# The low parts of W1 in an attention and mixture-of-experts kernel: subtractions on GpSimd in place of ScalarE copies and adding DMAs, for seven of sixteen halves

## The chip, the cores and the metric

The kernel runs on one core of a Trainium2 chip. The metric is the device time of one execution in microseconds (us); less is better. A core has five engines that run side by side, each with its own queue of instructions in a fixed order: TensorE (PE; PEld are its weight loads), VectorE (DVE), ScalarE (ACT), GpSimd (POOL) and SyncE (SP, which here only issues DMAs). SBUF is the on-chip memory that all of them read, PSUM the small one into which PE writes its sums, HBM the large one outside. DMAs issued by SP and by GpSimd go through different queues.

## The reference

Two parts follow each other. First a gated linear attention over 4 batches, 8 heads, 768 steps and 48 channels, then a mixture of 8 experts over the 3072 rows of 384 numbers that it gives. Tokens are assigned to experts greedily in the order of their logits, 384 to each expert:

```python
state = alpha[:, :, t, :, None] * state + np.einsum('bhd,bhe->bhde', k[:, :, t], v[:, :, t])
y[:, :, t] = np.einsum('bhd,bhde->bhe', q[:, :, t], state)
...
for e in range(E):
    mask = assigned == e
    h = np.maximum(x[mask] @ w1[e], 0.0)
    out[mask] = h @ w2[e]
```

W1 of an expert is 384 x 1024, W2 is 1024 x 384, all float32.

## The kernel before

The first 150 us are the attention and the first routing step. The change lies in what follows, the experts.

**The loop.** Experts are served in the order in which they fill up. Below they are called expert 0 to expert 7 by that order (i in the code), so "expert 1" is the second. Each has 8 blocks of 128 hidden units (q, `FB` = 8), in two halves of four: (i, 0) and (i, 1). `ffn1` (line 1056) computes a block's h from x and W1, nine matmuls; ScalarE then writes `hh`, the rounded positive part (line 1066), and VectorE `hl`, what the rounding left (line 1067). `ffn2` (line 1072), two blocks behind, multiplies both by W2 into `y`, nine matmuls.

**High and low parts.** PE takes float32 numbers here in a rounded form (`F32R`). So each weight half is split in two (`split`, line 977): a high part, the rounded copy, and a low part, the raw weight less the high part. Products are high by high, high by low and low by high. The tiles are `w1hi`, `w1lo`, `w2hi`, `w2lo`; each W1 half is 128 x 3 x 512, each W2 half 128 x 4 x 384, 768 KB both. ScalarE writes the high parts, two copies to a half (line 1005). The low parts come in two steps: ScalarE writes the *negated* rounded weight into `w1lo` or `w2lo`, and a DMA issued by GpSimd adds the raw weight to it in place (`low`, line 989, with `accum_op=OP.add`). Only the first half, (0, 0), has its `w1lo` from GpSimd's own subtraction, in four pieces of 128 columns (line 1023).

**The search.** While expert i is computed, the next expert's tokens are searched (`search`, line 712): five or six levels, each of them a chain from VectorE to PE and back. In a level VectorE makes `nd` (line 779) and `cmp` (line 683), PE counts with short matmuls into `rt` (lines 745 to 751), VectorE makes `need` and `gt` (lines 757 to 764), PE sums once more (line 772), VectorE takes `k` (line 776). At the end of a search stands a run of small VectorE operations (`q`, `ab`, `qe` and others through line 790), up to `sums`; then `extract` (line 914) makes the token indices `idx` (line 956), and GpSimd issues three gathers of rows, `xr` (line 963). PE transposes the rows into `xt` (line 1046), ScalarE copies them to `xh`, VectorE makes `xl`.

**What sets the order.** A scheduler puts the program into one order for each engine, from its own costs, and every engine keeps to it: PE waits at a search matmul even if the next expert matmul is ready, and a GpSimd instruction that waits holds all behind it. `tc.issue_after(x)` adds that an instruction comes after x on its queue. Rotating buffers bound how far ahead things go: three halves of each split tile, two experts of raw weights, five `yt` tiles for the stores of `y`, which GpSimd issues (line 1094).

## Time and profile before

| | |
|---|---|
| median of 3 runs | 412.92 us (411.97 to 413.25) |
| the profiled execution | 413.29 us, its span 411.6 us |
| clock granted to PE, mean | 0.991 |
| busy of the span: PE, DVE, ACT, POOL | 94%, 69%, 52%, 45% |
| instructions in the profile | 9897 |
| moved by DMA | 88.05 MB, of which 33.83 MB by GpSimd's queue |

The span is what the trace covers, from the first instruction to the last; what lies around it makes up the difference to the execution's time. A row of the timeline has the start in us from the span's begin, the duration in us, engine, line and operation, then written tile <- read tiles, shape and count; a bracket at its end tells how long the engine was idle before it and what ended that. A row of a group has count, busy time in us and mean ns. Rows of before carry the line numbers of the kernel before. Durations on GpSimd overlap each other somewhat: the next instruction's start is recorded before the one in front has ended.

### The profile page before, as it was taken

To read this page: it belongs to the slowest core of one execution; us is meant where nothing else is said; L and a number is where in the kernel's file an instruction comes from. 1 tells how busy PE (TensorE), PEld (TensorE's weight loads), DVE (VectorE), ACT (ScalarE), POOL (GpSimd) and SP (SyncE) were. 2 spreads that over 40 slices of the span, in tenths; PEclk is the share of its full clock that TensorE was granted. 3 is DMA by queue.
4 is the path that set the end of the run, shared out by engine and by line. 5 is a ranking of instruction groups with operands and counts; after the bars stand their busy time and mean duration, and the time that the engine had idled before them with its cause. 6 is when DMAs were issued, how large, how long until landed. Compare 5 with 4: busy or idle time off the path is not lost.

```text
span 411.6 us, 9897 instructions
## 1 busy us (share of the span) xinstructions
PE 385.0 (94%) x3775; PEld 340.6 (83%) x3775; DVE 283.3 (69%) x909; ACT 214.5 (52%) x382; POOL 186.8 (45%) x230
## 2 busy tenths in 40 slices
PE   6899999999999888898999998999999999999992
PEld 3788889887888556797798997899998999999992
DVE  8889997899994686687586796597796872312210
ACT  3456555654553015626639629529529539478211
POOL 5899988566851016213405506216126263614102
PEclk9899999999999999999999999999999999999998
DMA  8989898763020148789799999979999999999601
GB/s 274 378 284 309 276 311 230 245 200 105 22 79 30 50 151 204 164 204 262 206 220 323 200 282 274 213 252 278 210 298 226 197 303 327 247 305 202 155 0 58
DMA packets 43711, 88.05 MB, mean 214 GB/s; under 512 B 3856, under 2 KB 18192, under 8 KB 43664
## 3 DMA queue, kind: packets, MB, share of 16 engines
q0 software_dynamic: 11408, 33.83, 38.9%
q1 hardware_dynamic: 32256, 53.60, 38.5%
q8 instruction: 29, 0.48, 0.5%
q14 instruction: 18, 0.15, 0.1%
HBM read 53.59 MB, written 9.44 MB: 153 GB/s over the span
## 4 chain that ended last, share of the span: by engine, by line
PE 48%; DVE 16%; issue 15%; DMA 14%; POOL 3%; ACT 1%; POOLq 0%; SPq 0%; DVEq 0%
PE h L1062 12%; PE y L1082 11%; DMA w1r<-in_moe_w_dram 4%; PE xt L421 4%; PE y L484 4%; DMA w1lo<-w1r 4%; PE y L477 4%; PE s L433 4%; DMA xr<-x_dram,idx 3%; DMA w2lo<-w2r 3%; DVE te L393 3%; PE lg L502 2%; DVE tp L399 2%; PE rt L751 1%; PE st L445 1%
## 5 line engine op out<-in xcount | busy, mean ns | idle before, releaser
L1066 ACT ACTIVATE hh<-h 128x384 fp32r<-128x384 f32 x64 | 31.3, 488 | 85.3 <-PE h L1062 62.5
L1067 DVE SCALAR_TENSOR_TENSOR hl<-h,hh 128x384 fp32r<-128x384 f32 x64 | 35.4, 553 | 51.0 <-ACT hh L1066 50.7
L1082 PE MATMUL y<-w2hi,hh 128*128 128x384 f32 x192 | 66.6, 347 | 0.0
L1082 PE MATMUL y<-w2lo,hh 128*128 128x384 f32 x192 | 65.8, 343 | 0.4 <-DMA w2lo<-w2r 0.4
L1082 PE MATMUL y<-w2hi,hl 128*128 128x384 f32 x192 | 65.3, 342 | 0.0
L1094 POOL DMA_INDIRECT out_dram<-yt,idx x24 | 25.5, 1062 | 50.5 <-ACT yt L1087 46.8
L1062 PE MATMUL h<-xh,w1lo 128*128 128x384 f32 x192 | 46.9, 343 | 0.0
L1062 PE MATMUL h<-xh,w1hi 128*128 128x384 f32 x192 | 46.0, 342 | 0.6 <-ACT xh L1049 0.6
L1062 PE MATMUL h<-xl,w1hi 128*128 128x384 f32 x192 | 45.8, 342 | 0.0
L993 POOL DMA_DIRECT2D w1lo<-w1r x15 | 20.3, 1350 | 55.7 <-ACT w1lo L1005 40.1
L963 POOL DMA_INDIRECT xr<-x_dram,idx x24 | 26.2, 1092 | 40.4 <-DVE idx L956 26.2
L1062 PEld LDWEIGHTS h<-xh,w1hi 128*128 128x128 f32 x192 | 33.9, 188 | 4.4 <-issue 2.9
L403 POOL TENSOR_TENSOR kh<-rk,te 128x512 f32<-128x512 f32 (+1 forms) x24 | 29.4, 1226 | 17.1 <-DVE z L413 11.4
L1082 PEld LDWEIGHTS y<-w2lo,hh 128*128 128x128 f32 x192 | 36.3, 189 | 0.7 <-DMA w2lo<-w2r 0.7
L1082 PEld LDWEIGHTS y<-w2hi,hh 128*128 128x128 f32 x192 | 36.3, 189 | 0.0
L1082 PEld LDWEIGHTS y<-w2hi,hl 128*128 128x128 f32 x192 | 36.2, 189 | 0.1
L1062 PEld LDWEIGHTS h<-xl,w1hi 128*128 128x128 f32 x192 | 33.8, 189 | 0.5 <-DVE xl L1051 0.2
L1062 PEld LDWEIGHTS h<-xh,w1lo 128*128 128x128 f32 x192 | 33.9, 189 | 0.4 <-DMA w1lo<-w1r 0.3
L1005 ACT ACTIVATE w1hi<-w1r 128x768 fp32r<-128x768 f32 x32 | 26.8, 840 | 10.4 <-DMA w1r<-in_moe_w_dram 8.0
L435 ACT ACTIVATE sm<-s 128x1024 f32<-128x1024 f32 x24 | 24.6, 1026 | 13.9 <-PE s L433 13.4
L399 DVE TENSOR_TENSOR_SCAN tp<-al,z 128x512 f32<-128x512 f32 (+1 forms) x26 | 29.6, 1138 | 2.6 <-DVE z L413 0.5
L393 DVE TENSOR_TENSOR_SCAN te<-al,z 128x511 f32<-128x511 f32 (+2 forms) x26 | 30.8, 1186 | 0.5
(204 smaller groups left out, 833.8 us busy)
## 6 DMA issues: line engine op xcount, KB each, us to landing
w1r<-in_moe_w_dram SPq DMA_DIRECT2D x16, 768.0 KB, 7.7
w2r<-in_moe_w_dram SPq DMA_DIRECT2D x16, 768.0 KB, 10.0
w2lo<-w2r POOLq DMA_DIRECT2D x16, 768.0 KB, 10.4
w1lo<-w1r POOLq DMA_DIRECT2D x15, 768.0 KB, 8.0
al<-in_alpha_dram SPq DMA_DIRECT2D x24, 260.0 KB, 4.1
rk<-in_k_dram SPq DMA_DIRECT2D x24, 256.0 KB, 4.2
rq<-in_q_dram SPq DMA_DIRECT2D x24, 256.0 KB, 4.4
rv<-in_v_dram SPq DMA_DIRECT2D x24, 192.0 KB, 3.9
```

The lines of the kernel that those rows point to most:

```text
L393: nc.vector.tensor_tensor_scan(te.t[:, lo:top][:, ::-1], al.t[:, lo + 1:top + 1][:, ::-1], zb[:, lo + 1:top + 1][:, ::-1], al.t[:, 4 * C + ...
L399: nc.vector.tensor_tensor_scan(tp.t[:, lo:hi], al.t[:, lo:hi], zb[:, lo:hi], 1.0, op0=OP.mult, op1=OP.add)
L403: eng.tensor_tensor(out_.t[:, us].rearrange("p u c -> p (u c)"), x.t[:, lo:hi], f.t[:, lo:hi], op=OP.mult)
L435: add(A_, 1.05, lambda: nc.scalar.activation(sm.t, sc.t, AF.Copy), r=[(sc, 0), (sc, 1)], w=[sm])
L963: gathers[b] = last_gather[0] = nc.gpsimd.indirect_dma_start(out=XR[i][:, b], out_offset=None, in_=x_dram, in_offset=bass.IndirectOffsetOn ...
L993: return nc.gpsimd.dma_start(x.bitcast(F32), raw_, accum_op=OP.add, max_dma_last_dim=8192)
L1005: nc.scalar.activation(dst, src, AF.Copy, scale=scale)
L1062: F1[i, q] = nc.tensor.matmul(o, a[:, d], x[:, d], start=(n == 0), stop=(n == 3 * DB - 1))
L1066: HA[i, q] = nc.scalar.activation(hh, o, AF.Relu)
L1067: HL[i, q] = nc.vector.scalar_tensor_tensor(hl, o, 0.0, hh, op0=OP.max, op1=OP.subtract)
L1082: F2[i, q] = nc.tensor.matmul(Y[b], a[:, bs], w, start=(q == 0 and n == 0), stop=(q == FB - 1 and n == 2))
L1094: st_ = nc.gpsimd.indirect_dma_start(out=out, out_offset=bass.IndirectOffsetOnAxis(ap=IDX[i][:, b:b + 1], axis=0), in_=yt, in_offset=None)
```

## The change

A table `SUBTRACTED` names the halves whose `w1lo` is subtracted on GpSimd: (0, 0) as before, and now both halves of expert 1 and the first halves of experts 2 to 6. For those seven new halves ScalarE no longer writes the negated copy (two copies each) and no adding DMA for `w1lo` is issued; GpSimd subtracts four pieces each instead. The adding DMA for `w2lo` is issued between the second and the third piece (for (0, 0) ahead of the first, as before). The first piece comes after the latest issued gather in GpSimd's queue. The second halves of experts 2 to 6 and both halves of expert 7 stay with copies and DMAs.

```diff
+    SUBTRACTED = ((0, 0), (1, 0), (1, 1), *((i, 0) for i in range(2, E - 1)))
...
+        subtracted = (i, hf) in SUBTRACTED
...
-            copies(n, (hi1[ix_], w1r[ix_], 1.0), *([(lo1[ix_], w1r[ix_], -1.0)] * (not first)))
+            copies(n, (hi1[ix_], w1r[ix_], 1.0), *([(lo1[ix_], w1r[ix_], -1.0)] * (not subtracted)))
...
-        if first:
-            x = low(lo2, w2r)
+        if subtracted:
+            x = None
             for j in range(FB // 2):
+                if j == (0 if first else FB // 4):
+                    with tc.issue_after(x.ins) if x is not None else ExitStack():
+                        x = low(lo2, w2r)
                 c = slice(j * 128, (j + 1) * 128)
-                with tc.issue_after(x.ins):
+                with tc.issue_after((x or last_gather[0]).ins):
                     x = nc.gpsimd.tensor_sub(lo1[:, :, c], w1r[:, :, c], hi1[:, :, c])
         else:
             low(lo1, w1r)
```

The change also moves instructions on the engines. Three places follow. GpSimd's queue at expert 1, before: the gathers of expert 1 (`xr_2691`), the two adding DMAs of (1, 0), three stores of expert 0, the two adding DMAs of (1, 1), the gathers of expert 2.

```order
L963 DMA xr_2691<-x_dram_62,idx_2685 128x384 x3
L993 DMA w1lo_2697<-w1r_2641 128x3x512
L993 DMA w2lo_2699<-w2r_2642 128x1536
L1094 DMA out_0_dram<-yt_2770,idx_2185 3072x384
L1094 DMA out_0_dram<-yt_2775,idx_2185 3072x384
L1094 DMA out_0_dram<-yt_2780,idx_2185 3072x384
L993 DMA w1lo_2835<-w1r_2641 128x3x512
L993 DMA w2lo_2837<-w2r_2642 128x1536
L963 DMA xr_3179<-x_dram_62,idx_3173 128x384 x3
```

And the same place now (the lines of the changed kernel are some five further on):

```order
L964 DMA xr_2691<-x_dram_62,idx_2685 128x384 x3
L1028 TENSOR_TENSOR w1lo_2697<-w1r_2641,w1hi_2696 128x3x128 x2
L995 DMA w2lo_2699<-w2r_2642 128x1536
L1028 TENSOR_TENSOR w1lo_2697<-w1r_2641,w1hi_2696 128x3x128 x2
L1028 TENSOR_TENSOR w1lo_2836<-w1r_2641,w1hi_2835 128x3x128 x2
L1099 DMA out_0_dram<-yt_2771,idx_2185 3072x384
L1099 DMA out_0_dram<-yt_2776,idx_2185 3072x384
L1099 DMA out_0_dram<-yt_2781,idx_2185 3072x384
L995 DMA w2lo_2838<-w2r_2642 128x1536
L1028 TENSOR_TENSOR w1lo_2836<-w1r_2641,w1hi_2835 128x3x128 x2
L964 DMA xr_3181<-x_dram_62,idx_3175 128x384 x3
```

Two subtractions now stand ahead of each w2lo issue; the first two of (1, 1) stand ahead of expert 0's stores, the last two behind w2lo of (1, 1) and ahead of expert 2's gathers.

GpSimd's queue at expert 3, before (`xr_3655` are expert 3's gathers, `w1lo_3680` and `w2lo_3682` the half (3, 0), the last two rows the half (3, 1)):

```order
L1094 DMA out_0_dram<-yt_3267,idx_2685 3072x384
L993 DMA w1lo_3680<-w1r_3601 128x3x512
L963 DMA xr_3655<-x_dram_62,idx_3649 128x384 x3
L993 DMA w2lo_3682<-w2r_3602 128x1536
L993 DMA w1lo_3798<-w1r_3601 128x3x512
L993 DMA w2lo_3800<-w2r_3602 128x1536
```

And now:

```order
L1099 DMA out_0_dram<-yt_3270,idx_2685 3072x384
L964 DMA xr_3658<-x_dram_62,idx_3652 128x384 x3
L1028 TENSOR_TENSOR w1lo_3683<-w1r_3604,w1hi_3682 128x3x128 x2
L995 DMA w2lo_3685<-w2r_3605 128x1536
L1028 TENSOR_TENSOR w1lo_3683<-w1r_3604,w1hi_3682 128x3x128 x2
L995 DMA w1lo_3802<-w1r_3604 128x3x512
L995 DMA w2lo_3804<-w2r_3605 128x1536
```

The adding DMA of (3, 0) stood ahead of the gathers; its place is taken by subtractions behind them. The same holds at expert 4; at experts 2, 5 and 6 the gathers stood first already.

PE's queue at the start of expert 1, before: the third block of transposes, a search matmul, and at once the first blocks of h (`y_2315` is a block of expert 0's result).

```order
L1082 MATMUL y_2315<-w2hi,hl 128x384
L1046 MATMUL xt<-ident,xr 128x128 x3
L772 LDWEIGHTS one_84
L772 MATMUL rt<-gt_108,one_84 128x8
L1062 MATMUL h<-xh,w1hi 128x384 x4
L1062 MATMUL h<-xl,w1hi 128x384 x3
```

And now:

```order
L1051 MATMUL xt<-ident,xr 128x128 x3
L1087 MATMUL y_2315<-w2hi,hh 128x384
L1087 MATMUL y_2315<-w2lo,hh 128x384
L1087 MATMUL y_2315<-w2hi,hl 128x384
L1087 MATMUL y_2313<-w2hi,hh 128x384
L1067 MATMUL h<-xh,w1hi 128x384 x6
```

The third block of transposes stands some twelve matmuls earlier, with four matmuls of expert 0's y between it and the first h; between the second transposes and the next count of the search there are now 18 instead of 14 expert matmuls. On ScalarE the copies of the seven halves close up: at expert 2 the order `w1hi`, `w1lo`, `w1hi`, `w1lo`, `hh` becomes `w1hi`, `w1hi`, `w2lo`, `hh`. VectorE and SP have the same instructions, SP in the same order.

## The prediction

> **What bounds the kernel now.** First the page for its totals, then the busy time by stage from 191 us, where expert 1 begins. Columns: stretch, its length, then busy time of PE, PEld, DVE, ACT and POOL, the clock, the DMA share.

> ```profile
> PE 385.0 (94%) x3775; PEld 340.6 (83%) x3775; DVE 283.3 (69%) x909; ACT 214.5 (52%) x382; POOL 186.8 (45%) x230
> 191.00:225.00 34.00, 32.12 (x273) 29.24 (x271) 24.48 (x88) 19.45 (x33) 11.65 (x11) 1.00 0.96 243
> 225.00:258.00 33.00, 30.94 (x240) 28.10 (x238) 24.57 (x101) 20.09 (x33) 12.15 (x11) 1.00 1.05 251
> 258.00:400.00 142.00, 141.98 (x968) 133.96 (x969) 76.63 (x296) 80.92 (x137) 48.52 (x44) 1.00 0.93 231
> ```

> The matmuls bound every stage: from 258 to 400 us PE is busy 141.98 of 142 us. So removed ScalarE copies (ACT 52% busy) or GpSimd issues are worth nothing by themselves. What can be won are the holes of PE between 191 and 258 us, 1.88 us of them in the first row and 2.06 in the second. The timeline of PE names them; the bracket is the idle time before a row and what ended it.

> ```profile
> 196.99 0.98 PE L1062 MATMUL h<-xh,w1hi 128*128 128x384 f32 x4 [0.57 <-ACT xh L1049]
> 201.66 0.44 PE L1082 MATMUL y<-w2lo,hh 128*128 128x384 f32 x1 [0.42 <-DMA w2lo<-w2r]
> 221.11 0.17 PE L772 MATMUL rt<-gt,one 128*128 128x8 bf16 x1 [0.88 <-DVE gt L764]
> 252.65 0.17 PE L772 MATMUL rt<-gt,one 128*128 128x8 bf16 x1 [0.42 <-DVE gt L764]
> 257.90 1.02 PE L1046 MATMUL xt<-ident,xr 128*128 128x128 f32 x6 [1.64 <-DMA xr<-x_dram,idx]
> ```

> They add up to 3.93 us. Each ends in something that the change touches; the rest of this text takes them in turn, and then asks which new holes come.

> **The change part by part.** It removes 14 ScalarE copies and 7 adding DMAs, and adds 28 subtractions on GpSimd.

> ```profile
> L1005 ACT ACTIVATE w1lo<-w1r 128x768 fp32r<-128x768 f32 x30 | 25.1, 836 | 0.0
> 157.74 4.25 POOL L1023 TENSOR_TENSOR w1lo<-w1r,w1hi 128x384 fp32r<-128x384 f32 x4
> L1023 POOL TENSOR_TENSOR w1lo<-w1r,w1hi 128x384 fp32r<-128x384 f32 x4 | 4.3, 1364 | 0.0
> ```

> ScalarE loses 14 x 0.836 = 11.7 us. GpSimd loses seven issues. Its four present subtractions end 4.25 us after the first starts, and one alone takes 1.36, so each further one adds (4.25 - 1.36) / 3 = 0.96 us; 28 add 27 us. GpSimd is 45% busy and stays off the path in sum; its order matters, below. The low parts themselves come sooner, but none of PE's holes above ends in w1lo: worth 0.

> *The hole at 257.90.* It is the longest, and it is GpSimd's queue that makes it.

> ```profile
> 249.26 0.17 DVE L956 SCALAR_TENSOR_TENSOR idx<-xt,other 64x3 int32<-64x3 f32 x1
> 249.34 1.33 POOL L993 DMA_DIRECT2D w1lo<-w1r  x1 [13.84 <-ACT w1lo L1005]
> 250.98 1.07 POOL L963 DMA_INDIRECT xr<-x_dram,idx  x1 [0.30 <-issue]
> w1lo<-w1r POOLq DMA_DIRECT2D x1, 768.0 KB, 8.0
> xr<-x_dram,idx POOLq DMA_INDIRECT x3, 6.0
> 308.40 1.60 POOL L963 DMA_INDIRECT xr<-x_dram,idx  x1 [7.28 <-DVE idx L956]
> xr<-x_dram,idx POOLq DMA_INDIRECT x3, 3.6
> ```

> The first four rows are expert 3's (the last column of a DMA row is the median time to landing), the other two the gathers of expert 5. Expert 3's indices are ready at 249.43, but the adding DMA stands ahead of the three gathers, and lands at 249.34 + 8.0 = 257.3; the first gather lands just behind it, when the hole ends. Now the gathers go first, some 1.3 us sooner, with no 768 KB ahead of them in their queue. Where nothing of that kind was ahead, at expert 5, three gathers took 3.6 us in the median instead of 6.0. Landing then falls near 255, before PE wants them at 257.90 - 1.64 = 256.26. I take all 1.64; the low end is 0.9, if the weight loads in flight slow them as they do expert 2's.

> *221.11 and 252.65.* Both are VectorE's: ahead of the comparison `gt` stands `hl`, which waits for ScalarE's `hh`, and `hh` stands behind four copies.

> ```profile
> 218.88 0.83 ACT L1005 ACTIVATE w1lo<-w1r 128x768 fp32r<-128x768 f32 x1
> 219.61 0.47 ACT L1066 ACTIVATE hh<-h 128x384 fp32r<-128x384 f32 x1
> 220.12 0.56 DVE L1067 SCALAR_TENSOR_TENSOR hl<-h,hh 128x384 fp32r<-128x384 f32 x1 [1.08 <-ACT hh L1066]
> 251.65 0.56 DVE L1067 SCALAR_TENSOR_TENSOR hl<-h,hh 128x384 fp32r<-128x384 f32 x1 [1.23 <-ACT hh L1066]
> 224.85 0.82 PE L1046 MATMUL xt<-ident,xr 128*128 128x128 f32 x6
> 219.69 0.99 POOL L963 DMA_INDIRECT xr<-x_dram,idx  x1 [0.30 <-issue]
> xr<-x_dram,idx POOLq DMA_INDIRECT x3, 5.3
> ```

> In the new order two low copies go and one w2lo copy comes ahead of that `hh`: one copy less, 219.61 - 218.88 = 0.73 us. At 252.65 that covers the 0.42. At 221.11 it covers 0.73 of 0.88, but the next thing PE needs is expert 2's gathers: the middle one, issued at 219.69, landed 5.3 us later, at 225.0, and PE's transposes began at 224.85 with no hole. Coming 0.73 sooner, PE waits there for about 0.5. So 0.2 to 0.3 net; I take 0.3 (ends 0 and 0.73).

> *196.99 and 201.66.* The first two rows below belong to w2lo's late landing, the third gives PE's pace.

> ```profile
> 187.89 1.42 POOL L993 DMA_DIRECT2D w1lo<-w1r  x1 [1.06 <-ACT w1lo L1005]
> 190.46 0.92 POOL L993 DMA_DIRECT2D w2lo<-w2r  x1 [1.15 <-ACT w2lo L1005]
> 188.16 0.68 PE L1082 MATMUL y<-w2hi,hl 128*128 128x384 f32 x3
> ```

> PE's new order puts expert 1's third block of transposes four y matmuls ahead of the first h, and ScalarE has two copies fewer before `xh`. The present hole is the wait for `xh`, 0.57. Three such matmuls take 0.68 us, so four cover the 0.57 (low end 0). The w2lo's ScalarE copies come two places sooner, two subtractions stand ahead instead of an issue, and w1lo's transfer is no longer in front: issued between 189 and 190.6, landing well before 201.2: 0.42 (low end 0.2).

> Gains: 1.64 + 0.3 + 0.42 + 0.57 + 0.42 = 3.35 us (ends 1.2 and 3.93).

> *What it adds: holds of VectorE.* The search for the next expert alternates between VectorE and PE, in a fixed order. While GpSimd reads two tensors, VectorE's operations on two tensors seem to stand:

> ```profile
> 86.42 1.27 POOL L403 TENSOR_TENSOR qh<-rq,tp 128x512 f32<-128x512 f32 x1
> 86.51 1.20 DVE L568 TENSOR_TENSOR key<-m,sg 128x12 int32<-128x12 int32 x1
> L863 DVE TENSOR_TENSOR key<-m,sg 128x24 int32<-128x24 int32 x4 | 0.7, 176 | 0.0
> 161.63 0.41 DVE L779 SCALAR_TENSOR_TENSOR nd<-dig,k 128x24 bf16<-128x24 bf16 x1
> ```

> The tiny `key` took 1.20 us beside GpSimd's product and ended with it; its larger sibling alone takes 0.176. `nd` at 161.63 lies under the last present subtraction and ends 0.05 us behind it (157.74 + 4.25 = 161.99). [...]

> In each search level only `nd` and `cmp` read two SBUF tensors (`need`, `gt`, `hl` and `k` have an operand in PSUM, and I take them as free), so the question is whether they meet a subtraction. The subtractions stand behind the gathers, two, one DMA issue, two. For expert 5:

> ```profile
> 311.58 0.95 POOL L963 DMA_INDIRECT xr<-x_dram,idx  x1 [0.30 <-issue]
> 313.82 0.24 DVE L779 SCALAR_TENSOR_TENSOR nd<-nd,k,dig 128x24 bf16<-128x24 bf16 x1
> 314.10 0.56 DVE L683 TENSOR_TENSOR cmp<-nd,iota 128x768 bf16<-128x768 bf16 x1
> 314.74 0.44 PE L745 MATMUL rt<-o,cmp 128*128 128x32 bf16 x8
> 317.14 0.24 DVE L779 SCALAR_TENSOR_TENSOR nd<-nd,k,dig 128x24 bf16<-128x24 bf16 x1
> ```

> The gathers' issues end at 312.53; the first two subtractions run to 312.53 + 2 x 0.96 = 314.45, the other two from about 315.4 to 317.3. `nd` at 313.82, 0.24 us long here against the 0.41 above, is held 0.6 us; PE reads `cmp` 0.08 us after its end, so the hole is nearly 0.6. The next `nd`, moved to 317.7, is clear. The same reckoning from the indices of experts 2, 3 and 4 gives holds of up to 0.5, 0 and 0.2, of which expert 2's lies under its wait for the gathers: 0 together, high end 1.0 each. For (1, 0) the long hold falls on a `cmp` that PE does not want before the gathers land; two later ones meet a level that now has four more matmuls in front: 0.2. For (1, 1) the last two subtractions come behind w2lo's issue and meet the dense end of a search:

> ```profile
> 206.50 0.89 POOL L993 DMA_DIRECT2D w2lo<-w2r  x1 [2.23 <-ACT w2lo L1005]
> 208.83 0.23 DVE L790 TENSOR_SCALAR q<-nd,k 128x24 f32<-128x24 bf16 x1
> ```

> With the 0.99 us of the two earlier holes gone, the issue stands at 205.5, the subtractions behind it at 206.4 to 208.3, and `q`, with several operations on two SBUF tensors after it, at 207.8: held 0.5 (ends 0 and 1.9). Expert 6's four come when VectorE has only the last choice left, with slack in PE's order: 0. Holds: 0.6 + 0.2 + 0.5 = 1.3 us (ends 0 and 5.8, a full subtraction in each of six halves).

> Queued behind the subtractions are the w2lo adding DMAs (1 to 2 us later than without them, about as the w1lo issues held them before) and expert 0's three stores, behind two subtractions that wait for ScalarE; the ring of five yt tiles covers those, and no engine waits for a store before the end.

> Sum: 3.35 - 1.3 = 2.05 us less. The profiled execution took 413.29 us, 0.37 above the median of 412.92; from the median: 410.9.

> **The rivals.** *Holds cost nothing:* VectorE slips between the subtractions. For it: the holds foreseen are few and hang on tenths of a microsecond. Against: the 1.20 us row. All of the holes go: 412.92 - 3.9 = 409.0. *The holes move:* the gathers of experts 2 and 3 land as late as now, since the DMA share is 0.96 and 1.05 in those two stages, so PE only reaches them sooner; 0.57 + 0.42 remain won, against 1.3 of holds: 412.92 + 0.3 = 413.2. *Slower by holds:* the phases fall worse by half a microsecond, and a full subtraction holds `nd` in each of the six halves from (1, 0) to (5, 0): 5.8 - 3.35 = 2.5 more, 415.4. It decides from 3.35 / 0.96, that is when more than three of the six are hit in full. For it: PE reads `cmp` 0.08 us behind its end, so there is no slack to take a hold up; against it: the rhythm worked out above. [...]

> **How the numbers follow.** Forecast 0.45, nothing from the holds 0.2, moved holes 0.2, slower 0.15. The forecast's own ends (gain 1.2 to 3.93, holds 0 to about 3) put a fifth of it within 1.2 us of no change. The range runs from 408.5, half a microsecond (the runs' own spread) below the best case, to 415.0, which takes in the moved holes and part of the slower case. 0.3% (1.2 us) is about what a measurement of this kernel can tell from no change. Faster: 0.36 + 0.2, with a little of the moved holes: 0.57; same 0.24; slower 0.19.

> **What would show it.** In the changed profile the rows at 257.90 and 252.65 lose their brackets, expert 3's gathers come directly behind `idx`, and expert 2's transposes gain a wait of about 0.5. `nd` and `cmp` rows beside the subtractions grow from 0.24 to up to 1.2 us, at expert 5 and at the end of the search within (1, 1), with a PE wait on `cmp` or `sums` right after. Wrong it is if no such row grows, if gathers still end PE's longest hole, or if such rows appear at every expert.

## The result, and the profile after

The changed kernel took 430.01 us (median of 4 runs, 429.25 to 432.85), the kernel before, run beside it, 413.09 us (411.97 to 413.71): a ratio of 1.0425, 95% interval 1.0373 to 1.0478. It is 4% slower, where 410.9 us was forecast and 415.0 was the upper end. The profiled execution of after took 429.72 us with a span of 427.4, 15.8 us longer than before's 411.6. Here and below, medians are over all executions of a kernel, while ratios leave out those more than 1.5% above the fastest of the same kernel.

Of the page of after, the busy time of PE and the row with the granted clock in 40 slices (10.7 us each; 9 is full):

```profile
PE 392.9 (92%) x3775; PEld 347.5 (81%) x3775; DVE 297.8 (70%) x909; ACT 205.6 (48%) x368; POOL 205.3 (48%) x251
...
PEclk9699999999999999999998998899999899999998
```

PE has the same 3775 matmuls and is busy 7.9 us longer with them; besides, it is idle for longer. The clock row tells where the first comes from: 8s from the 22nd slice on. The timeline of PE in after names the idle time, between 186 and 400 us:

```profile
191.21 0.55 PE L1051 MATMUL xt<-ident,xr 128*128 128x128 f32 x3 [1.23 <-DMA xr<-x_dram,idx]
192.40 0.96 PE L749 MATMUL rt<-o,cmp 128*128 128x8 bf16 x24 [0.64 <-DVE cmp L684]
221.38 0.17 PE L773 MATMUL rt<-gt,one 128*128 128x8 bf16 x1 [0.44 <-DVE gt L765]
225.91 0.57 PE L752 MATMUL rt<-o,cmp 128*128 128x16 bf16 x12 [2.68 <-DVE cmp L684]
264.38 0.44 PE L746 MATMUL rt<-o,cmp 128*128 128x32 bf16 x8 [2.87 <-DVE cmp L684]
298.12 0.44 PE L746 MATMUL rt<-o,cmp 128*128 128x32 bf16 x8 [2.74 <-DVE cmp L684]
330.65 0.44 PE L746 MATMUL rt<-o,cmp 128*128 128x32 bf16 x8 [2.87 <-DVE cmp L684]
```

The five holes of before are gone, or halved in the case of `gt` at 221. In their place stand four new ones, one at each of the experts 2 to 5, all ended by the same thing: `cmp`, the search's comparison on VectorE. They add up to 11.16 us. What VectorE and GpSimd did ahead of the one at 298.12, in order of time:

```profile
292.69 0.56 DVE L1072 SCALAR_TENSOR_TENSOR hl<-h,hh 128x384 fp32r<-128x384 f32 x1
292.70 2.00 POOL L1028 TENSOR_TENSOR w1lo<-w1r,w1hi 128x384 fp32r<-128x384 f32 x2
294.31 0.88 DVE L780 SCALAR_TENSOR_TENSOR nd<-nd,k,dig 128x24 bf16<-128x24 bf16 x1
294.63 1.02 POOL L995 DMA_DIRECT2D w2lo<-w2r  x1
295.22 2.84 DVE L684 TENSOR_TENSOR cmp<-nd,iota 128x768 bf16<-128x768 bf16 x1
295.27 2.36 POOL L1028 TENSOR_TENSOR w1lo<-w1r,w1hi 128x384 fp32r<-128x384 f32 x2
```

`nd` meets the tail of the first pair of subtractions and takes 0.88 us instead of 0.24. The w2lo issue stands between the pairs, but `nd` ends only when half of it is over, and `cmp` follows at once: it begins 0.05 us ahead of the second pair, which runs to 297.63, and ends at 298.06. It is held through both subtractions, not through one. `hl` at 292.69 lies beside a subtraction too and takes its usual 0.56 us; it reads one of its two tensors from PSUM. The rows that group all comparisons of this shape, first before, then after:

```profile
L683 DVE TENSOR_TENSOR cmp<-nd,iota 128x768 bf16<-128x768 bf16 x16 | 8.9, 557 | 0.5
```

```profile
L684 DVE TENSOR_TENSOR cmp<-nd,iota 128x768 bf16<-128x768 bf16 x16 | 15.8, 988 | 0.5
L1072 DVE SCALAR_TENSOR_TENSOR hl<-h,hh 128x384 fp32r<-128x384 f32 x64 | 35.4, 554 | 47.2 <-ACT hh L1071 46.8
```

The 16 comparisons take 6.9 us more in all, three times 2.3; the fourth held one, at expert 2, has another shape. The busy time by stretch shows the second price, behind each of the four holes (last three columns: clock, DMA share, GB/s):

```profile
225.91:230.00 4.09, 4.09 (x28) 3.71 (x28) 1.73 (x6) 0.10 (x1) 3.03 (x3) 0.58 0.98 192
264.38:270.40 6.02, 6.02 (x27) 5.62 (x28) 2.85 (x10) 0.98 (x2) 2.21 (x3) 0.50 1.07 190
298.12:302.10 3.98, 3.98 (x25) 3.87 (x26) 1.75 (x8) 0.77 (x2) 1.75 (x2) 0.62 1.06 192
330.65:336.00 5.35, 5.34 (x34) 4.74 (x35) 2.41 (x10) 1.22 (x2) 1.75 (x2) 0.68 1.07 191
```

PE is busy all the time there, at a clock of 0.50 to 0.68; before had 1.00 from 258 to 400. What is lost is the length times the missing share: 1.7 + 3.0 + 1.5 + 1.7 = 7.9 us. The sum: 11.2 of holes, 7.9 of clock and 0.64 for the small hole at 192.40, less the 3.5 us of holes that went (0.57 + 0.42 + 0.42 + 1.64, and 0.88 - 0.44), makes 16.2 us; the span grew by 15.8. (Expert 3's gathers would be in time without PE's new delays too: in e3 below, where no long hole comes before them, PE does not wait for them either.)

The theory to be tested was: while GpSimd subtracts, reading two tensors, VectorE's operations that read two tensors from SBUF stand until the row of subtractions ends; PE, which has the search's matmul next in its order, idles; and an idle time of that length drops the granted clock, to the 0.50 to 0.68 of the rows above. The rivals: the new orders of PE and ScalarE; late transfers; any work of GpSimd; expert 1's own holds as the trigger.

### The profile page after: what moved, and what is told of

Read it like the earlier page. It is cut to its first block, busy times and chain, and to the rows that moved or that the text cites. A ratio compares the mean times of both kernels' runs of the same rounds, so it can differ in the third digit from the quotient of the medians.

```text
span 427.4 us, 9908 instructions
## 1 busy us (share of the span) xinstructions
PE 392.9 (92%) x3775; PEld 347.5 (81%) x3775; DVE 297.8 (70%) x909; ACT 205.6 (48%) x368; POOL 205.3 (48%) x251
## 4 chain that ended last, share of the span: by engine, by line
PE 63%; DVE 18%; issue 8%; DMA 4%; ACT 3%; POOL 1%; SPq 1%; POOLq 0%; DVEq 0%; ACTq 0%
PE y L1087 19%; PE h L1067 19%; DVE cmp L684 4%; PE xt L422 4%; PE y L485 4%; PE y L478 4%; PE s L434 4%; PE lg L503 2%; DVE te L394 2%; PE rt L752 2%; DVE tp L400 1%; DMA w1r<-in_moe_w_dram 1%; DMA al<-in_alpha_dram 1%; PE xt L1051 1%; PE st L446 1%
## 5 line engine op out<-in xcount | busy, mean ns | idle before, releaser
L1087 PE MATMUL y<-w2hi,hh 128*128 128x384 f32 x192 | 68.3, 356 | 0.0
L1087 PE MATMUL y<-w2lo,hh 128*128 128x384 f32 x192 | 67.8, 353 | 0.0
L1087 PE MATMUL y<-w2hi,hl 128*128 128x384 f32 x192 | 67.5, 353 | 0.0
L1099 POOL DMA_INDIRECT out_dram<-yt,idx x24 | 24.1, 1002 | 65.9 <-ACT yt L1092 63.0
L1067 PE MATMUL h<-xh,w1lo 128*128 128x384 f32 x192 | 47.1, 345 | 0.0
L1067 PE MATMUL h<-xh,w1hi 128*128 128x384 f32 x192 | 46.9, 347 | 0.0
L1067 PE MATMUL h<-xl,w1hi 128*128 128x384 f32 x192 | 46.3, 345 | 0.0
L404 POOL TENSOR_TENSOR kh<-rk,te 128x512 f32<-128x512 f32 (+1 forms) x24 | 29.4, 1225 | 17.4 <-DVE z L414 11.8
L1087 PEld LDWEIGHTS y<-w2hi,hl 128*128 128x128 f32 x192 | 37.6, 196 | 0.1
L1087 PEld LDWEIGHTS y<-w2lo,hh 128*128 128x128 f32 x192 | 37.5, 195 | 0.0
L1087 PEld LDWEIGHTS y<-w2hi,hh 128*128 128x128 f32 x192 | 37.5, 195 | 0.0
L684 DVE TENSOR_TENSOR cmp<-nd,iota 128x768 bf16<-128x768 bf16 (+4 forms) x36 | 36.6, 1027 | 1.1
L1028 POOL TENSOR_TENSOR w1lo<-w1r,w1hi 128x384 fp32r<-128x384 f32 x32 | 35.8, 1226 | 2.5 <-ACT w1hi L1007 2.4
L1067 PEld LDWEIGHTS h<-xh,w1hi 128*128 128x128 f32 x192 | 34.3, 191 | 2.5 <-issue 1.6
L1067 PEld LDWEIGHTS h<-xl,w1hi 128*128 128x128 f32 x192 | 34.2, 191 | 0.5 <-DVE xl L1056 0.2
L1067 PEld LDWEIGHTS h<-xh,w1lo 128*128 128x128 f32 x192 | 34.4, 191 | 0.1
L437 POOL TENSOR_SCALAR_AFFINE_SELECT sm<-sm 128x1024 f32<-128x1024 f32 x24 | 26.2, 1092 | 11.5 <-ACT sm L436 11.1
## 6 DMA issues: line engine op xcount, KB each, us to landing
w1r<-in_moe_w_dram SPq DMA_DIRECT2D x16, 768.0 KB
w2r<-in_moe_w_dram SPq DMA_DIRECT2D x16, 768.0 KB
w2lo<-w2r POOLq DMA_DIRECT2D x16, 768.0 KB
w1lo<-w1r POOLq DMA_DIRECT2D x8, 768.0 KB
```

What stands on the lines that cost most here:

```text
L404: eng.tensor_tensor(out_.t[:, us].rearrange("p u c -> p (u c)"), x.t[:, lo:hi], f.t[:, lo:hi], op=OP.mult)
L437: add(G_, 1.15, lambda: nc.gpsimd.affine_select(sm.t, sm.t, pattern=[[0, 8], [1, C]], compare_op=OP.is_ge, fill=0.0, base=0, channel_multi ...
L684: nc.vector.tensor_tensor(words(dst, nt, js), keyed(d, nt, js), each(iotas[t], nt, js), op=OP.is_ge)
L1028: x = nc.gpsimd.tensor_sub(lo1[:, :, c], w1r[:, :, c], hi1[:, :, c])
L1067: F1[i, q] = nc.tensor.matmul(o, a[:, d], x[:, d], start=(n == 0), stop=(n == 3 * DB - 1))
L1087: F2[i, q] = nc.tensor.matmul(Y[b], a[:, bs], w, start=(q == 0 and n == 0), stop=(q == FB - 1 and n == 2))
```

## The experiments

The kernel before ran beside each group of them, on other chips, where its median was 415.1 to 417.1 us; ratios are against those runs.

**Expert 1 alone (e1).**

```
-SUBTRACTED = ((0, 0), (1, 0), (1, 1), *((i, 0) for i in range(2, E - 1)))
+SUBTRACTED = ((0, 0), (1, 0), (1, 1))
```

> The subtractions of expert 1's two halves stay, those of experts 2 to 6 go back to copies and adding DMAs. Theory (VectorE's comparisons are held while GpSimd subtracts, experts 2 to 5): the four holes of 2.7 to 2.9 us and the slow clock behind them go; the forecast gains at 196.99 and 201.66 (0.57 + 0.42) and part of 221.11 (0.3) stay, so 411 to 413 us, against 413.1 before. Rival A (the new order of the first experts' work on PE and ScalarE costs the time): most of the 17 us stays, 425 us or more. Rival B (expert 1's own holds, where one VectorE operation took 2.72 instead of 0.35 us, set off the rest): some 3 to 5 us stay, 416 to 418.

Measured: 0.9987 (0.9935 to 1.004), the four holes gone. What is left on PE of its kind is 0.49 us at expert 1:

```profile
190.60 0.56 PE L749 MATMUL rt<-o,cmp 128*128 128x8 bf16 x12 [0.49 <-DVE cmp L684]
...
251.94 0.17 PE L773 MATMUL rt<-gt,one 128*128 128x8 bf16 x1 [0.96 <-DVE gt L765]
256.64 0.55 PE L1051 MATMUL xt<-ident,xr 128*128 128x128 f32 x3 [1.12 <-DMA xr<-x_dram,idx]
```

The new order of the first experts' work is not the cause. Nor does a gain stand clear of the noise (the interval reaches from 2.7 us less to 1.7 more): the `gt` hole and the gathers' hole of expert 3 are still there, since its adding DMA stands ahead of the gathers again.

**All but expert 1 (e9).**

```
+SUBTRACTED = ((0, 0), *((i, 0) for i in range(2, E - 1)))
```

> The changed kernel without the subtractions of expert 1's two halves (copies and adding DMAs there); those of experts 2 to 6 stay. Theory: the four holes stay, with what follows them, 15 to 19 us above before: 429 to 436 on a chip where before takes 413 to 417. Rival (the holes of experts 2 to 5 are set off by expert 1's held operation, 2.72 us at 187.49, or by its new order): most of the loss goes, 420 or less.

Measured: 1.0417 (1.0346 to 1.0488), with holes of 2.72, 2.93, 2.72 and 2.92 us. Two of them:

```profile
264.46 0.43 PE L746 MATMUL rt<-o,cmp 128*128 128x32 bf16 x8 [2.93 <-DVE cmp L684]
...
328.37 0.44 PE L746 MATMUL rt<-o,cmp 128*128 128x32 bf16 x8 [2.92 <-DVE cmp L684]
```

The whole loss sits in experts 2 to 6; the two runs together rule out expert 1 as its cause or trigger.

**One tensor instead of two (e3).**

```
-x = nc.gpsimd.tensor_sub(lo1[:, :, c], w1r[:, :, c], hi1[:, :, c])
+x = nc.gpsimd.tensor_scalar(lo1[:, :, c], hi1[:, :, c], 0.0, None, op0=OP.mult)   # halves of experts 1 to 6
```

> The changed kernel with each of its 28 new subtractions replaced by w1hi times 0.0 (GpSimd reads one tensor from SBUF instead of two; W1's low parts of those halves come out as zero, so part of the product is left out). Every engine's order stays that of the changed kernel. Theory (two tensors read by GpSimd and two by VectorE hold each other): the held comparisons fall from 2.8 to 3.8 us back to 0.55 to 0.95, the four holes and the slow clock go, 410 to 412 us. Rival (any GpSimd operation on SBUF holds them): 425 to 430. Rival (order, late transfers): 430, nothing changes.

Measured: 0.9957 (0.9913 to 1.0), no hole on PE over 1.34 us between 186 and 400 us. Comparisons and GpSimd's new operations in this run, then a comparison that lies wholly beside a pair of them:

```profile
L684 DVE TENSOR_TENSOR cmp<-nd,iota 128x768 bf16<-128x768 bf16 x16 | 10.1, 632 | 0.5
L1028 POOL TENSOR_SCALAR w1lo<-w1hi 128x384 fp32r<-128x384 f32 x28 | 37.3, 1448 | 1.5 <-ACT w1hi L1007 1.3
...
284.06 0.74 DVE L684 TENSOR_TENSOR cmp<-nd,iota 128x768 bf16<-128x768 bf16 x1
283.48 2.70 POOL L1028 TENSOR_SCALAR w1lo<-w1hi 128x384 fp32r<-128x384 f32 x2
```

GpSimd works longer than in after, at the same places of the same queue, and with the same order of instructions on every other engine; the comparisons take 0.63 us on average instead of 0.99. So it is not the order, not the transfers and not GpSimd's being busy; what went is GpSimd's reading of a second tensor from SBUF. One thing stays open: the edit also makes the operation another instruction, a multiplication by a number instead of a subtraction of tensors, and no run tells the count of tensors from the kind of instruction. The run also gives an estimate of what the change would have won without the holds: 0.0043 x 415.9 = 1.8 us (0 to 3.6).

**Three in a row (e4).**

```
-if j == (0 if first else FB // 4):
+if j == (0 if first else 1 if i > 1 else FB // 4):
```

> The changed kernel with the w2lo issue of experts 2 to 6 behind the first subtraction instead of the second, so that one subtraction stands alone and three follow each other. Theory (a comparison that meets a row of subtractions is held to the end of the last): it now ends 0.4 to 0.6 us behind the third, some 0.3 to 1 us later than behind the second: each of the four holes 3.0 to 3.9 us, 431 to 435 us. Rival (it is held only by the subtraction during which it began): holes of 1 us or less, 417 to 422.

Measured: 1.0274 (1.0158 to 1.0391), 430.32 us against 430.01 of after on its own chip; holes of 1.79, 2.90, 2.94 and 3.11. At expert 3, VectorE, GpSimd and PE:

```profile
258.72 3.78 DVE L684 TENSOR_TENSOR cmp<-nd,iota 128x768 bf16<-128x768 bf16 x1
258.76 3.31 POOL L1028 TENSOR_TENSOR w1lo<-w1r,w1hi 128x384 fp32r<-128x384 f32 x3
262.55 0.44 PE L746 MATMUL rt<-o,cmp 128*128 128x32 bf16 x8 [2.90 <-DVE cmp L684]
```

The comparison is held through all three, 3.78 us, and ends 0.43 us behind the third. The rival, one subtraction at most, is out. The time did not rise with it, against the expectation of up to 5 us more; that the ratio lies below after's 1.0425 shows no gain either, since it rests on three runs between 425.6 and 430.7 us and the two intervals overlap. In the trace the three begin sooner, so that the hole grows by 0.03 to 0.24 us only at experts 3 to 5, and at expert 2, where `cmp` meets the single one first, it is 0.89 us shorter.

**A break between them (e5).**

```
+if i > 1 and j % 2:
+    with tc.issue_after(x.ins):
+        x = nc.gpsimd.memset(lo1[:, :, c].bitcast(F32), 0.0)
 with tc.issue_after((x or last_gather[0]).ins):
     x = nc.gpsimd.tensor_sub(lo1[:, :, c], w1r[:, :, c], hi1[:, :, c])
```

> The changed kernel with a GpSimd memset (it only writes) between the two subtractions of each pair of experts 2 to 6; nothing else moves on any engine. Theory (a comparison is held by GpSimd's reading of two tensors as long as such operations follow each other without a break): it gets through at the memset, so it is held by one subtraction, about 1 us instead of 2.3; the holes shrink to some 1.0 to 1.5 us, TensorE's clock stays at 1.00 behind them as it did behind the hole of 1.64 us of before, and the time is 413 to 419 us. Rival (the operation that was held waits until GpSimd has done all that is queued, or a writing operation holds it as well): holes of 3 us or more, 430 to 436.

Measured: 1.0121 (1.0035 to 1.0207), that is a median of 421.5 us on this chip, and by the ratio 5 us above before (1.5 to 8.6); some two thirds of the loss are gone. At expert 4, GpSimd and VectorE, then PE's two longest waits for `cmp`:

```profile
287.09 1.96 DVE L780 SCALAR_TENSOR_TENSOR nd<-nd,k,dig 128x24 bf16<-128x24 bf16 x1
287.63 1.36 POOL L1031 TENSOR_TENSOR w1lo<-w1r,w1hi 128x384 fp32r<-128x384 f32 x1
288.57 0.78 POOL L1029 MEMSET w1lo<- 128x384 f32 x1
...
289.70 0.44 PE L746 MATMUL rt<-o,cmp 128*128 128x32 bf16 x8 [1.50 <-DVE cmp L684]
320.45 0.43 PE L746 MATMUL rt<-o,cmp 128*128 128x32 bf16 x8 [2.37 <-DVE cmp L684]
```

The held operation ends at 289.05, with the single subtraction (288.99), while the memset still runs (288.57 to 289.35): here an operation that only writes lets VectorE through. The holes are 1.5 us where one subtraction is met and 2.37 where `nd` meets one and `cmp` the next; of these it was only the longest behind which the clock fell. The time lies 2 us above the end of what the theory gave, 419; before itself takes 4 us longer on this chip than on that of after, so the difference says nothing about that hole.

**One expert (e6).**

```
+SUBTRACTED = ((0, 0), (4, 0))
```

> The kernel before with subtractions for the first half of one expert only, the fifth (number 4), in the place where the changed kernel has them. Theory (each expert pays by itself: a hole of some 2.7 us, and 1.5 to 3 us of clock at 0.50 behind it): 4 to 6 us above before, one hole. Rival (the loss needs the whole reordered stretch, or holes that follow each other): no change within 1 us, or more than 10 us.

Measured: 1.0089 (1.0048 to 1.0131), 3.7 us (2.0 to 5.5), about a fifth of what after lost. In the profiled execution, the hole and the 2 us behind it:

```profile
290.87 0.44 PE L746 MATMUL rt<-o,cmp 128*128 128x32 bf16 x8 [2.75 <-DVE cmp L684]
290.87:292.90 2.03, 2.03 (x20) 1.99 (x21) 1.19 (x5) 0.06 (x1) 1.75 (x2) 1.00 1.03 194
```

The hole is that of after, 2.75 us, and the clock stayed at 1.00. So the drop does not follow each such hole; the last section sets them side by side. This was the fastest of this kernel's ten runs, 416.52 us of a median of 419.58.

**VectorE subtracts (e7).**

```
+if not first:
+    nc.vector.tensor_sub(lo1[:, :, c], w1r[:, :, c], hi1[:, :, c])
+    continue
```

> The changed kernel with the 28 new subtractions on VectorE instead of GpSimd. Theory (the loss is GpSimd's and VectorE's reading at the same time, not the subtraction, the missing copies or the gathers ahead of the low parts): no comparison is held over its usual duration; VectorE gets 28 x about 0.55 = 15 us of work, most of it beside PE's; 409 to 415 us. Rival (the new order of transfers and copies costs the time): 425 or more. A third possibility: VectorE's extra work stands in the search's way, up to 4 x 0.55 us at each of six halves, 415 to 422.

Measured: 1.0137 (1.005 to 1.0224), 5.7 us above before. No comparison is held and the four holes of after are gone, which agrees with the theory; but the time is that of the third possibility. The longest hole now ends in expert 2's gathers, whose indices are ready at 220.19 instead of 217.46 in before:

```profile
226.23 0.33 PE L1054 MATMUL xt<-ident,xr 128*128 128x128 f32 x1 [2.89 <-DMA xr<-x_dram,idx]
```

**The search's matmul later (e8).**

```
+if 3 <= i < E - 1 and t == (2 if i > 3 else 0):
+    es_.enter_context(tc.issue_after((F2[i - 2, FB - 2] if i > 3 else F1[1, FB - 1]).ins))
```

> The changed kernel with the search's matmul that met each of the four holes queued later on PE: for expert 3's search behind the last first-layer matmul of expert 1, for the searches of experts 4 to 6 behind the second-to-last block of y, some 14 to 17 matmuls (2.5 to 2.9 us) further back. The subtractions stay. Theory (hold, then PE without other work, then slow clock): comparisons are still held 2.8 us or more, but PE works on meanwhile; the holes shrink below 1 us, the clock stays at 1.00 there, and of the 17 us 10 to 16 go: 414 to 420 us. Rival (the search itself is the critical path, so that a later search gives the time back in late weights): the holes move to the next wait for weights or gathers, 424 us or more. Rival (the subtractions slow PE itself): 428 to 430.

Measured: 1.0182 (1.0128 to 1.0236), more than half of the loss gone, and neither theory as written: at experts 3 to 5 no operation of VectorE is held any more, since the search is now elsewhere when the subtractions run. At expert 2 a held `cmp` remains, with a hole of 1.81 us. Waits of 0.6 to 1.5 us for gathers came at experts 2 to 6, and a new hole at expert 1, which the edit does not touch. VectorE and PE there:

```profile
188.88 4.40 DVE L684 TENSOR_TENSOR cmp<-dig,iota 128x3072 bf16<-128x3072 bf16 x1
193.34 0.96 PE L751 MATMUL rt<-o,cmp 128*128 128x8 bf16 x24 [3.26 <-DVE cmp L684]
```

The same comparison in after, with the pair of subtractions beside it:

```profile
190.60 1.74 DVE L684 TENSOR_TENSOR cmp<-dig,iota 128x3072 bf16<-128x3072 bf16 x1
191.19 2.99 POOL L1028 TENSOR_TENSOR w1lo<-w1r,w1hi 128x384 fp32r<-128x384 f32 x2
```

There it began 0.59 us ahead of the pair, in e8 0.45 (the pair at 189.33): 0.14 us decides over 2.7.

**Gathers ahead of the adding DMA, without subtractions (e2, e10, e11).** The prediction's largest gain was the hole of 1.64 us at expert 3, made by the queue order. These buy the order alone: for experts 3 to 6, and for expert 3 only.

```
-if i == 0 or i < 3 and not hf:
+if i == 0 or i < E - 1 and not hf:     # e2
+if i == 0 or i < 4 and not hf:         # e10; e11 with SUBTRACTED of e1 as well
```

> Copies and adding DMAs as before; only the adding DMA of w1lo for the first halves of experts 3 to 6 is queued behind that expert's gathers instead of ahead of them. The orders of the other engines are those of before. If the hole of 1.64 us at 257.90 came from that queue order, as the prediction said, and the later w1lo isn't missed: 411.5 us. If w1lo, issued some 3 us later and landing 8 us after that, becomes the wait: 414 to 417. If the loss of the changed kernel came from gathers standing ahead of the low parts (rival): 420 or more.

> The kernel before with one queue order changed: expert 3's three gathers ahead of its adding DMA of w1lo, nothing else. If the hole of 1.64 us at 257.90 is that queue's and comes back nowhere, as the prediction's largest term had it: 1.6 us less than before, ratio 0.996. Rival (the raw weights are read some 4 us later, so that a later expert's weights arrive later, as with all four experts moved): no gain or up to 2 us more, ratio 1.000 to 1.005.

> Expert 1's subtractions (whose long hold met no search step that PE waited for long) and expert 3's gathers ahead of its adding DMA; no subtraction where a search runs later. If the prediction's gains of expert 1 (0.57 + 0.42 + 0.3) and of expert 3's gathers (1.1 to 1.6) hold without the later holds: 2 to 3 us less than before, ratio 0.993 to 0.995, faster than both kernels. Rival (they are given back in the next wait): ratio 0.998 to 1.003.

Measured: 1.0048 (1.0009 to 1.0086), 1.0024 (0.9986 to 1.0062) and 1.0085 (1.0051 to 1.0119). In all of them the hole at expert 3 is gone, and the gain is given back one expert on. In e10, ScalarE's first copy of the next weights, PE's hole behind it, and the traffic ahead:

```profile
278.64 0.85 ACT L1005 ACTIVATE w1hi<-w1r 128x768 fp32r<-128x768 f32 x1 [4.59 <-DMA w1r<-in_moe_w_dram]
283.82 0.17 PE L772 MATMUL rt<-gt,one 128*128 128x8 bf16 x1 [2.64 <-DVE gt L764]
270.00:272.00 2.00, 2.00 (x14) 1.95 (x14) 1.97 (x14) 0.49 (x1) 0.00 (x0) 1.00 0.98 206
```

The same in before:

```profile
276.36 0.85 ACT L1005 ACTIVATE w1hi<-w1r 128x768 fp32r<-128x768 f32 x1 [0.62 <-DMA w1r<-in_moe_w_dram]
270.00:272.00 2.00, 2.00 (x14) 1.80 (x13) 1.97 (x15) 0.17 (x1) 0.00 (x0) 1.00 0.33 114
```

In before the adding DMAs have all but drained by 270 us (DMA share 0.33) when the next weights are asked for; queued behind the gathers they still run (0.98), and the weights are there 2.3 us later, although SP asked for them 1.06 us earlier (270.45 against 271.51): 8.2 us pass from their issue to the copy that reads them, against 4.9. So it is not that buffers came free later, as the rival had it; the transfer itself took longer. In e2 the same hole is 2.45 us, and its clock serves the theory's second half, for no subtraction is near it:

```profile
284.11 0.17 PE L772 MATMUL rt<-gt,one 128*128 128x8 bf16 x1 [2.45 <-DVE gt L764]
284.10:286.10 2.00, 1.99 (x7) 1.99 (x7) 0.97 (x3) 2.00 (x4) 1.94 (x2) 0.50 0.84 246
```

So here idle time of PE was enough for the slow clock. e11 was slower by 3.5 us, and has a further cause: expert 1's comparison was held, as in e8.

```profile
190.44 4.46 DVE L684 TENSOR_TENSOR cmp<-dig,iota 128x3072 bf16<-128x3072 bf16 x1
194.96 0.96 PE L749 MATMUL rt<-o,cmp 128*128 128x8 bf16 x24 [3.17 <-DVE cmp L684]
```

It began 0.51 us ahead of the pair, against 0.59 in after: even expert 1's subtractions are safe only by a tenth of a microsecond. No version beats both kernels: e3, the only one that is likely ahead of before, leaves out the low parts.

## Why the prediction was wrong, point by point

*The gains* came about as forecast: 3.5 us of holes removed in the trace of after, against 3.35. But taken without the holds, in e3, they are worth 1.8 us (0 to 3.6), since smaller waits follow. The wait of about 0.5 us foreseen for expert 2's transposes is in neither trace. And the 1.64 of the gathers seems to be a gain only because the subtractions also take 768 KB per half off the queues: with the adding DMA kept and moved (e10), it was given back by 2.64 us at the next expert. The ends of the gain, 1.2 and 3.93, do not come out of the ends of its terms, which add up to 1.52 (252.65 has no low end of its own, so with its 0.42) and 3.78; this has no part in the miss.

*The holds* are the step that failed: "Holds: 0.6 + 0.2 + 0.5 = 1.3 us (ends 0 and 5.8, a full subtraction in each of six halves)". In place of 1.3 us they made holes of 11.8 (11.16 at experts 2 to 5, 0.64 at expert 1). The mechanism was the right one, as far as e3 can tell: two readers of two tensors. (In e3, where GpSimd reads one tensor, the `cmp` at 284.06 is held by 0.18 us, against 2.3, and the 16 comparisons take 1.2 us more than in before, 10.1 against 8.9, where after's take 6.9 more. That VectorE's operations with an operand in PSUM go free was assumed; `hl` at 292.69, 0.56 us beside a subtraction with a mean of 554 ns over all 64, bears it out.) Three things in its sizing were not:

- The upper end took one subtraction, 0.96 us, as the most that an operation can be held. It is the whole row: two held `cmp` for 2.3 us, three for 3.2 (e4). Even one alone cost more than 0.96 where the held operation's row begins ahead of it: `nd` 1.7 (e5).
- The reckoning of phases followed `nd` and called what comes behind it clear. `nd` was held 0.64 us at expert 4, where up to 0.2 was reckoned, and by that very hold `cmp`, 0.03 us behind it, came into the next pair: of the 0.57 us between the pairs (294.70 to 295.27) `nd` used 0.49 to finish.
- The second half of expert 1, with 0.5 us of the sum, shows no held row in the search behind it; (1, 0) holds `o`, one of the operations ahead of a search, which takes 2.72 us instead of 0.35, at no more than 0.64 us for PE.

*The clock* was no term at all, and is the second step that failed. The prediction quoted 1.00 for every stage and took PE's pace as given; 7.9 us of the loss, half of it, is work behind the holes at 0.50 to 0.68 on average.

*The slower rival* had the side, the place and the mechanism, and with 415.4 a seventh of the loss, for it multiplied the wrong unit (one subtraction) and knew nothing of the clock. The sentence on what would show the forecast wrong, "such rows appear at every expert", is what the profile shows. *Holds cost nothing* is refuted by the rows at experts 2 to 5, and *the holes move* by the vanished ones; moved holes are what e2 and e10 have.

## What to carry to other kernels

Before work goes to an engine whose operations can hold those of one on the critical path, as GpSimd's pairs of subtractions held `cmp` for 2.3 us here, count how long its operations run without a break, not how long one takes, and ask which short operations of the other engine follow each other into that stretch: a step of 0.56 us that PE waits for can cost 2.8. A hole of PE can cost more than its length: three of the four in after cost 1.5 to 1.7 us of clock on top, and one 3.0. And a queue order that removes a wait should be followed to the next transfer that it delays (by 2.3 us in e10).
